# Weighing by W on three engines' paths, grouped q products and a split at column 384 in a spectral and MLP kernel

## The chip, the cores and the metric

The kernel runs on one core of one Trainium2 chip. The metric is the device time of one execution in microseconds; the time of a version is the median of several executions.

The core has a matrix engine (TensorE, PE in the profile, with its weight loads as PEld), a vector engine (VectorE, DVE), an engine for activations (ScalarE, ACT), GpSimd (POOL) and an engine that only issues transfers here (SyncE, SP). Matrix products land in PSUM, which has 8 banks of 128 partitions by 512 float32 columns. DVE and ACT copy them from there into the on-chip memory SBUF; GpSimd does not take operands from PSUM in this kernel.

## The reference

x has 2048 rows (S) and 512 columns (D), in bfloat16. Two kinds of layer, A and B, run twice in turn.

```
def _A_ref(x, w_r, w_i):
    X = rfft2(x)                     # over S and D
    X = X * (w_r + 1j * w_i)         # the weighing by W
    return irfft2(X)

def _B_ref(x, w1, w2, w3, w4):
    h = gelu(layernorm(x) @ w1)
    hs = shifted(h) @ w2             # four column groups, rows shifted by -1, +1, -2, +2
    x1 = x + hs
    return x1 + gelu(layernorm(x1) @ w3) @ w4

x = x + A(layernorm(x)); x = x + B(layernorm(x))
x = x + A(layernorm(x)); x = x + B(layernorm(x))
```

w1 and w2 are 512 by 512, w3 is 512 by 1792, w4 is 1792 by 512.

## The kernel before, in words

Row s of x is kept as partition p and index q, s = 16 p + q, so there are 16 blocks q of 128 rows. The state x stays in SBUF. The Fourier transforms are products with tables: `O` (front) transforms over p, `d` over the columns, `q` over q, then each coefficient is weighed by W (`p`), and `b`, `D`/`C` and `P` go back over q, over the columns and over p. `take` steps, one after each product, copy PSUM to SBUF: `G`/`L` after `O`, `t` after `d`, `x` after `q`, `m`/`l` after `b`, `Y` after `D`/`C`. They are `activation` copies on ACT or casts on DVE.

The spectrum is cut into 16 blocks b. Blocks 2 to 13 go through d, q and p in pairs (a unit of two), blocks 0, 1, 14 and 15 alone. A pair's d, q products, their copies (TV and X) have 1024 columns, a single's have 512. The weighing reads X and W from SBUF and writes 2048 products (1024 for a single): each value of X by the real and by the imaginary plane of W. PB holds the result. `product_slot` gives the place; the last two units reuse places of the first. A product of the q step is over 64 partitions, two at a time side by side; all other products are over 128.

After the spectral part `a` adds to x, `s` and `r` form the statistics of the rows, `n` normalises, `T` transposes by a transfer (issued by SP), `v` and `h` are w1 and its gelu, `u` is w2, `f` adds, `k`, `R`, `o`, `U` are again squares, statistics, normalising and transposing, `E` adds to x, `w`, `g`, `W` and `A` are w3, gelu, w4 and the addition to x. In layer 1 `B`, `j`, `S`, `J`, `Q` then compute the next layer's statistics and scale the table T for each q, and `O` and `G` begin the next spectral part among the w4 products. In layer 2 `y` stores the result.

Nothing is scheduled by a tool at run time or at build time: three strings, ORDER_0 (the first front), ORDER_A (layer 1) and ORDER_B (layer 2), list every step. A letter is the step, the number its index, a last letter the engine (A for ACT, V for DVE, P for GpSimd), and .n the first PSUM bank of the product. Every engine runs its own instructions in the order in which they stand in the strings, and waits for what they read. So `p4V` is the weighing of unit 4 on DVE, and everything listed behind it for DVE waits with it. `Xn` issues n products of zeros. On POOL stand also the small instructions of the row statistics (`r`, `c`, `R`, and `M`), and the issue of some table loads: `load_tables` at `f2`, and `load_rest` after ORDER_0. The first transfer of `load_rest` doubles the first quarter of W.

The last rows of w4's products are cut in two halves of 256 columns (HALVES, `columns`): in layer 1 row index 14 (W14 and W24), in layer 2 row index 10 (W10 and W20).

The weighing before (line 577) and the cut (line 740):

Of the kernel before, what the change touches and what calls it, by code (L numbers as in the profile page):

```python
# [522 lines left out]

def layer(K, last):
# [52 lines left out]
    def weigh(u, eng):  # L577
        n = len(UNITS[u])
        small = n == 1 and u not in LATE[last]
        pab[u] = t = product_slot(PB, n_pab, small, n)  # L580
        (nc.vector if eng == "V" else nc.gpsimd).tensor_tensor(t, X.pop(u)[:, 0:2 * n].unsqueeze(1).to_broadcast([P, 2, 2 * n, 256]),  # L581
                                K.W[:, :, 2 * u:2 * u + 2 * n, 1:257], op=ALU.mult)

# [156 lines left out]
    def columns(n):  # L740

        if n not in (HALVES[last], HALVES[last] + 10):
            return n, slice(0, D)
        return HALVES[last], slice(0, D // 2) if n == HALVES[last] else slice(D // 2, D)

    def w4(n):
        r, d = columns(n)
        g, i = divmod(r, 4)
        ps["W", n] = o = banks(K, 1)[:, 0, 0:d.stop - d.start]
        for t in range(14):  # L750
            nc.tensor.matmul(o, lhsT=gT[g][:, t, i * P:(i + 1) * P], rhs=K.w4[:, t, d],  # L751
                             start=(t == 0), stop=(t == 13))

    def add_x2(n):
        r, d = columns(n)
        x = K.x[:, ROWS[r], d]
        nc.vector.tensor_tensor(x, ps.pop(("W", n)), x, op=ALU.add)  # L757
# [107 lines left out]
D3.1 C3 Y0V P3.6 P2.0 a3 P0.3 a2 a0 D2.5 P1.4 Y3A C2 a1 s3 s2 D5.1 C5 P7.0 s0 P6.3 Y2V P4.4 s1 r0 Y5A a7 D6.6 a6 e0 i0
M0 C6 P5.5 D7.0 s7 C7 a4 P11.4 s6 P10.2 Y6A P12.3 n1V n0V a5 s4 s5 r1 n2V n3V T0 D4.6 C4 a10 a11 Y7A P15.5 P14.2 e1 i1
Y4A P8.1 M1 n7V n4A n6V n5V s10 c0 T1 a8 P13.4 a12 s8 P9.6 a9 s11 a15 s9 a14 v0.0 h0 r2 c2 T3 v1.6 n11V h1 n8V T2 n9V
v3.2 n10V T5 v2.0 a13 h3 u0.3 s14 h2 u3.2 c1 f3 s15 u1.5 T4 u2.4 s12 s13 f0 k0 v5.1 f1 E1V r3 c3 E3V n14A n12V n13V
n15V T6 v4.6 f2 h5 T7 u4.0 h4 u6.2 f4 E2V f6 k2 k3 E0V k1 R0 u5.1 u7.5 f7 f5 k4 E4V k6 E6V v6.2 h6 v7.5 k7 o1V h7 k5
R1 o3V E5V o2V u15.7 o5A o0V f15 k15 E7V u8.0 f8 u14.1 f14 E8V U1 u12.6 f12 k12 U0 u13.4 f13 E13V u10.0 o4V o7A U2 k14  # L870
k13 o6V f10 E10V u11.3 f11 R3 k10 U3 w0.6 k8 k11 u9.0 f9 E9V o13V k9 E12V o12V U6 w2.2 E14V g2 o14A w4.0 R2 g4 o10A g0
w3.2 E15V w5.0 g5 E11V w6.4 g6 o15V g3 w1.0 g1 w8.6 W1.3 o11V W3.2 W0.0 o9V o8V A1 B1 j1 A3 B3 W2.1 w10.2 j3 g8 A0 B0
A2 j0 B2 j2 w13.6 S0 Q1A Q0V w7.4 Q2A Q3V g10 w12.0 U7 g7 O0.4 g12 U5 G0A w9.2 g9 w11.0 U4 G0V O1.2 g13 g11 W5.5 G1A
A5 B5 w15.6 G1V I1V I0V W6.0 W7.1 A6 B6 W4.3 j5 w17.4 A7 g15 g17 w14.0 B7 j7 w18.5 A4 g18 w16.2 B4 g16 w19.4 j4 j6 S1
Q4V Q6V Q7V O3.2 Q5V g14 g19 w20.6 g20 W10.0 A10 B10 G3A G3V O2.5 j10 I3V G2A W9.4 A9 B9 j9 W11.1 A11 G2V B11 j11 W8.0
w23.2 A8 g23 w21.6 g21 w27.0 B8 j8 w22.5 S2 Q10V Q9V g27 Q8V Q11V I2V w24.2 O4.0 g22 g24 G4A w26.5 g26 w25.2 g25 G4V
I4V W12.6 A12 B12 W13.3 W15.7 j12 S12 J12 A13 B13 j13 W24.3 S13 Q12V J13 Q13V A15 B15 W14.1 j15 A24 O5.2 B24 S15 J15
A14 B14 j14 Q15V G5A S14 O6.0 J14 O15.4 G6A Q14A O14.6 L6A L15A G14A G5V I5V G15A L14A
# [5 lines left out]
b7.6 m9A m12A m5V b14.2 b6.3 V12.7 m8A V14.0 m11V m10A m14A m6A V15.1 l15A m7V D3.2 l13A D2.4 l12V l14V C3 C2 D1.6 Y2V
C1 Y3A P7.1 a7 P6.0 a6 Y1A D0.2 s7 C0 Y0A s6 P4.1 a4 s4 P5.7 a5 P2.6 P3.1 s5 a3 s3 r1 D4.2 P0.7 a2 P1.1 s2 D7.4 a0 C7
C4 a1 e1 i1 s0 D5.0 C5 Y4A s1 M1 n4V D6.6 n5V C6 r0 n6V Y6A P8.3 P9.2 e0 n7V Y5V P10.6 P12.7 i0 a9 Y7A T2 P13.0 T3 M0
n2A n0V n1V T0 P11.1 s9 P15.2 a8 s8 n3V c0 a10 s10 a11 s11 P14.4 r2 a15 v3.5 v2.1 c1 a12 h3 T1 a13 a14 v0.3 h2 c2 n10V
h0 s13 v1.6 h1 u3.5 n11V s15 n8V s14 n9V s12 f3 k3 E3V u1.4 f1 u0.0 E1V u2.3 f2 k1 T5 T4 v5.6 r3 v4.2 k2 f0 h5 u4.0 k0
n13V n12V h4 E0V n15V T6 n14V f4 k4 u7.6 f7 R0 E4V c3 u6.1 f6 o3A u5.7 f5 E5V o1A E7V k7 E2V k5 T7 E6V v6.4 h6 o0V U0
v7.0 h7 k6 R1 u14.5 f14 k14 o2A u12.0 o4A f12 u8.1 U1 f8 E8V k12 o7V u10.4 f10 o5A u15.7 f15 k10 u13.0 k15 f13 u11.1  # L890
E10V k13 R3 k8 E14V u9.5 w2.2 o6A g2 w0.6 f11 E15V E12V E13V o13A w5.1 f9 U2 w6.4 o15A g0 o12V U3 k11 k9 g5 R2 w1.6 g1
w3.0 g3 w4.2 g4 E11V U6 g6 W0.0 W2.4 o11V W3.1 W1.5 o8V o14A U7 E9V w22.2 o10A g22 o9V U4 U5 w23.6 g23 A0 y0 w24.2 g24
A3 A1 w11.0 A2 y2 y1 w7.6 g7 w12.2 w21.4 g11 y3 w27.0 g21 w26.4 w9.6 g26 w8.4 g9 g12 w25.6 g8 g25 g27 W14.2 W15.4 A15
# [33 lines left out]
```

## Time and profile before

| what | us |
|---|---|
| median of 3 runs | 347.03 (346.26 to 347.15) |
| the profiled execution | 346.95 |
| its span, first to last instruction | 345.0 |
| PE busy | 337.0 (2191 matmuls) |
| PEld busy | 188.2 |
| DVE busy | 175.8 |
| ACT busy | 197.4 |
| POOL busy | 60.8 |
| granted TensorE clock | 0.999 |

The execution's stages in the trace, with the busy time of three engines in each:

| stage | from, to | length | DVE | ACT | POOL |
|---|---|---|---|---|---|
| load of x, first front | 0 to 19.2 | 19.2 | | | |
| layer 1: d, q, weighing, b | 19.2 to 38.1 | 18.9 | 17.30 | 17.89 | 4.59 |
| layer 1: D, C, P | 38.1 to 52.6 | 14.5 | 12.63 | 12.66 | 3.74 |
| layer 1: MLP, next front | 52.6 to 179.5 | 126.9 | 63.36 | 60.95 | 22.89 |
| last front of layer 2 | 179.5 to 183.4 | 3.9 | 3.39 | 3.29 | 0.00 |
| layer 2: d, q, weighing, b | 183.4 to 202.1 | 18.7 | 17.44 | 16.87 | 0.00 |
| layer 2: D, C, P | 202.1 to 216.7 | 14.6 | 11.64 | 13.14 | 3.94 |
| layer 2: MLP | 216.7 to 341.5 | 124.8 | 35.96 | 58.56 | 18.91 |
| last addition and store | 341.5 to 345.0 | 3.5 | 0.42 | 0.00 | 0.00 |

How to read it. An engine's busy time is the time in which one of its instructions was running. The end of a matmul is modelled in the profile, and neighbours overlap, so that PE's busy time covers short gaps. A chain of waits is followed back from the last instruction to what released each step. Instructions of ACT and DVE that follow each other directly overlap a little: what one costs its engine is the distance between two starts, which is shorter than its duration. The two stages of d, q, weighing and b are called the spectral stages below.

### The profile page before, as it was taken

The numbers are of one execution on the slowest core, as the hardware profiler recorded it, in microseconds if no ns is written. First come the engines' busy times: TensorE is split into PE (matmuls) and PEld (weight loads), VectorE is DVE, ScalarE is ACT, GpSimd is POOL, SyncE is SP. The second block draws the span as 40 slices with busy tenths as digits, with TensorE's granted clock in tenths as the row PEclk, the third lists the DMA queues.
The fourth block names the chain that finished last, engine by engine and source line by source line (L and its number), as shares of the span: only waits on it lengthen the run. The fifth ranks groups of instructions, "written<-read, shape, count | busy, mean of one in ns | idle before, by whom it ended". The sixth has DMA issues, their size and how long they took to land.

```text
span 345.0 us, 5696 instructions
## 1 busy us (share of the span) xinstructions
PE 337.0 (98%) x2191; PEld 188.2 (55%) x2191; DVE 175.8 (51%) x421; ACT 197.4 (57%) x361; POOL 60.8 (18%) x157
## 2 busy tenths in 40 slices
...
DMA packets 45258, 24.59 MB, mean 71 GB/s; under 512 B 34944, under 2 KB 42240, under 8 KB 45232
## 3 DMA queue, kind: packets, MB, share of 16 engines
...
q8 instruction: 17, 0.28, 0.3%
q10 hardware_dynamic: 240, 0.10, 0.1%
...
## 4 chain that ended last, share of the span: by engine, by line
PE 80%; ACT 12%; DMA 3%; DVE 2%; issue 2%; SPq 0%; ACTq 0%; DVEq 0%
PE ps L751 28%; PE ps L731 28%; PE ps L696 8%; PE ps L680 7%; PE ps L403 3%; ACT hT L154 3%; ACT xn L290 3%; ACT X L154 3%; ACT Y L154 2%; PE ps L612 1%; ACT TV L154 1%; DMA T<-tab_T 1%; DMA x_state<-in_A_x_dram 1%; PE ps L550 1%; DMA xT<-xn 1%
## 5 line engine op out<-in xcount | busy, mean ns | idle before, releaser
L738 ACT ACTIVATE gT<-ps 128x1024 bf16<-128x1024 f32 x56 | 55.8, 1022 | 87.8 <-PE ps L731 78.1
L731 PE MATMUL ps<-xT,w 128*128 128x512 bf16 x448 | 99.0, 379 | 0.0
L751 PE MATMUL ps<-w,gT 128*128 128x512 bf16 (+1 forms) x476 | 98.6, 366 | 0.0
L757 DVE TENSOR_TENSOR x_state<-ps,x_state 128x512 bf16<-128x512 f32 (+1 forms) x34 | 22.2, 659 | 115.4 <-PE ps L751 115.4
L751 PEld LDWEIGHTS <-gT 128*128 128x128 bf16 x476 | 46.5, 98 | 50.1
L731 PEld LDWEIGHTS <-w 128*128 128x128 bf16 x448 | 43.7, 98 | 52.1 <-DMA xT<-xn 0.2
L704 DVE SCALAR_TENSOR_TENSOR xn<-xn,ln_c,ps 128x512 bf16<-128x512 bf16 x32 | 23.2, 745 | 12.6 <-PE ps L696 7.2
L680 PE MATMUL ps<-xT,w 128*128 128x512 bf16 x128 | 28.8, 379 | 0.1
L696 PE MATMUL ps<-w,hT 128*128 128x512 bf16 x128 | 28.9, 379 | 0.0
L278 DVE BATCH_NORM_STATS2 ln_st<-x_state 128x6 f32<-128x512 bf16 (+1 forms) x31 | 20.4, 668 | 4.4 <-DMA x_state<-in_A_x_dram 3.9
L290 ACT ACTIVATE junk<-xn 128x512 bf16<-128x512 bf16 x32 | 19.8, 622 | 3.2 <-DVE xn L704 3.2
L648 DVE SCALAR_TENSOR_TENSOR x_state<-ps,x_state 128x512 bf16<-128x512 f32 x32 | 20.5, 686 | 0.9 <-PE ps L640 0.8
L696 PEld LDWEIGHTS <-hT 128*128 128x128 bf16 x128 | 12.4, 98 | 15.4 <-ACT hT L687 0.8
L680 PEld LDWEIGHTS <-w 128*128 128x128 bf16 x128 | 12.3, 98 | 15.2 <-DMA xT<-xn 0.9
L290 ACT ACTIVATE xn<-x_state 128x512 bf16<-128x512 bf16 x32 | 19.9, 627 | 0.7 <-DVE x_state L648 0.4
L581 DVE TENSOR_TENSOR PB<-X,W 128x2048 bf16<-128x2048 bf16 (+1 forms) x20 | 19.4, 1009 | 0.4 <-ACT X L154 0.2
L296 POOL TENSOR_SCALAR ln_mv<-ln_s 128x4 f32<-128x4 f32 x16 | 5.1, 317 | 80.2 <-DVE x_state L648 74.1
L687 ACT ACTIVATE hT<-ps 128x512 bf16<-128x512 f32 x32 | 17.2, 601 | 1.1 <-PE ps L680 1.0
L592 PE MATMUL ps<-TR,PB 128*128 128x128 bf16 x256 | 16.5, 219 | 0.1
L640 PE MATMUL ps<-Y,Tinv 128*128 128x256 bf16 x128 | 16.1, 272 | 0.4 <-ACT Y L154 0.3
L612 PE MATMUL ps<-G,hT 128*128 128x256 bf16 x128 | 15.6, 273 | 0.3 <-ACT hT L154 0.2
L592 PEld LDWEIGHTS <-PB 128*128 128x128 bf16 x256 | 14.7, 98 | 2.1 <-issue 1.5
...
## 6 DMA issues: line engine op xcount, KB each, us to landing
w<-in_B_w_dram SPq DMA_DIRECT2D x2, 1792.0 KB, 14.5
...
```

What stands on the lines that cost most here:

```text
L154: K.nc.scalar.activation(dst, src, ACT.Copy, bias=0.0, scale=1.0)
L278: self.K.nc.vector.bn_stats(self.st[i][:, int(k)], src)
L290: K.nc.scalar.activation(out, src, ACT.Square, bias=0.0, scale=D ** -0.5, accum_out=self.s[:, i, 1:2])
L592: nc.tensor.matmul(o[:, k0 * P:(k0 + 1) * P], lhsT=pab[u][:, k, 2 * (b - u) + h, f * P:(f + 1) * P], rhs=K.TR[:, k:k + 2, 2 * b + h], star ...
L648: nc.vector.scalar_tensor_tensor(K.x[:, q, :], ps.pop(("P", q)), 1.0, K.x[:, q, :], op0=ALU.mult, op1=ALU.add, accum_out=ln[g].s[:, i, 0:1])
L680: nc.tensor.matmul(o[:, i], lhsT=K.w1[:, t, j * P:(j + 1) * P], rhs=xT[g][:, :, t, :], start=(t == 0), stop=(t == 3))
L696: nc.tensor.matmul(o, lhsT=K.hT[:, j, st:st + P], rhs=K.w2[:, j, :], start=(j == 0), stop=(j == 3))
L704: nc.vector.scalar_tensor_tensor(xn[:, q, :], xn[:, q, :], ln[q // 4].c[:, q % 4:q % 4 + 1], ps.pop(("u", n)), op0=ALU.mult, op1=ALU.add, ...
L731: nc.tensor.matmul(o[:, i], lhsT=K.w3[:, c, t * P:(t + 1) * P], rhs=xT3[g][:, :, c, :], start=(c == 0), stop=(c == 3))
L738: nc.scalar.activation(gT[g][:, 2 * j:2 * j + 2, :], ps.pop(("w", k)), ACT.Gelu_apprx_tanh, bias=0.0, scale=1.0)
L751: nc.tensor.matmul(o, lhsT=gT[g][:, t, i * P:(i + 1) * P], rhs=K.w4[:, t, d], start=(t == 0), stop=(t == 13))
L757: nc.vector.tensor_tensor(x, ps.pop(("W", n)), x, op=ALU.add)
```

## The change

The weighing gets a third form. With the letter D it reads the q product straight from PSUM on DVE, once for each block of the unit, and the copy X of that unit falls away. The letter P, which the code had, puts the weighing of X on GpSimd. The cut of the last rows moves from column 256 to 384, in both layers. Then all three orders are new.

```
@@ weigh @@
         pab[u] = t = product_slot(PB, n_pab, small, n)
+        if eng == "D":
+            o = ps.pop(("q", u))
+            for i in range(n):
+                nc.vector.tensor_tensor(t[:, :, 2 * i:2 * i + 2], o[:, :, i * 256:(i + 1) * 256].unsqueeze(1).to_broadcast([P, 2, 2, 256]),
+                                        K.W[:, :, 2 * (u + i):2 * (u + i) + 2, 1:257], op=ALU.mult)
+            return
         (nc.vector if eng == "V" else nc.gpsimd).tensor_tensor(t, X.pop(u)[:, 0:2 * n].unsqueeze(1).to_broadcast([P, 2, 2 * n, 256]),
                                 K.W[:, :, 2 * u:2 * u + 2 * n, 1:257], op=ALU.mult)
@@ columns @@
-        return HALVES[last], slice(0, D // 2) if n == HALVES[last] else slice(D // 2, D)
+        return HALVES[last], slice(0, CUT[last]) if n == HALVES[last] else slice(CUT[last], D)
@@ constants @@
 HALVES = (14, 10)
+CUT = (384, 384)
@@ ORDER_0 @@
-s1 s0 i1 i0 s3 S0 s2 s5 J0 Q1A Q0A s7 i2 i3 s4 S1 J1 O0.4 s9 f2 s6 Q2V i7 i4 i6 s10 Q3A O1.0 S2 J2 G0A Q4V s11 s8 Q5A
-i10 O2.2 i11 Q6A f3 Q7A O3.6 i8 S3 s12 J3 Q10V s13 i12 G2A Q11A i13 O5.4 s14 Q8A S4 J4 G3A Q9V s15 G5A O4.2 Q12V i14
-Q13V O6.6 L5A i15 S5 J5 Q15V O8.4 Q14V G4A G6A L6A O7.2 G7A L7A G1V G8V L8V
+s1 s0 i1 i0 S0 s2 s5 J0 Q0A Q1A s4 s7 s6 i4 f2 O0.4 i7 i6 S2 s3 J2 i2 s9 Q6V Q7V O3.0 i3 s11 S1 J1 s10 Q4A Q2A Q5A G3A
+s8 i11 i10 i8 s12 f3 O2.2 Q3P O1.6 S3 J3 Q11P s13 i12 Q10A O5.0 s15 G0A i13 Q8A Q9P S4 G2A s14 i15 J4 Q12V i14 O4.4 S5
+J5 Q15V G1A G5V Q13P O6.2 L5A O8.0 Q14V O7.6 G4A G6V G7A L7A G8V L6V L8V
@@ ORDER_A @@
-d0.6 d2.0 N0 d1.4 t0A q0.2 t1A d4.6 t2V x0A t4A p0V q1.4 q2.0 d10.2 d6.6 x1A q4.4 t10A x2V d8.0 q10.2 t6A p1V x4V
-d14.6 p2V t8A q6.4 x10A q8.0 p4V b3.7 d12.2 x6A b0.4 t14A m3V d15.7 b4.5 p6V t12A q12.2 b5.6 t15V x8A b2.7 m4A m0A m5A
-p10V q14.0 x14A b7.5 b1.6 x12A b10.4 m10A b6.0 m6A q15.1 p8V b11.3 p14V x15A b14.4 m1A p12V m7A V12.0 b9.1 m9A m2V
...
+d2.2 t2V d0.6 t0A d1.0 d4.4 N0 q0.6 t1A q2.2 d6.0 x0V p0V q1.6 t4A q4.4 x2A d10.2 t6A d8.0 p1D b1.6 p2P t10A b0.7
+q10.2 p4D m0V t8A q6.0 d14.4 m1A d12.6 x10A t14V p10V x6A d15.2 t12A p6V b2.5 b4.3 m4A q14.0 q12.6 x14A q8.3 p12D b3.0
+m2A b10.1 b11.5 x8A b7.4 t15A p14P q15.2 b5.6 b14.7 m10A b6.1 m11A b12.5 m7A m5A m3A b13.4 m6A p8V b8.6 m12A p15D b9.0
...
+a3 s3 P6.0 a2 s2 P1.1 P0.6 a1 a0 s1 P7.2 D2.4 C2 D5.6 s0 a7 s7 D7.2 C5 Y2V P5.1 r0 e0 i0 a6 Y5A a5 D4.4 s6 s5 P4.0 M0
+n3V a4 n0V n2P s4 n1P D6.6 C7 C6 Y6A P11.0 T1 C4 P10.1 Y7V P15.2 r1 e1 a11 P12.3 i1 M1 n7V T0 Y4A n6V s11 n5A T3 P13.6
...
+u6.5 f1 k1 u5.6 c2 E3V f7 E7V E2V f4 k2 R0 o2V f6 o3A v6.2 h6 v7.0 h7 f5 E1P E6V o1P k4 E0V o0V u12.4 k6 k7 k5 R1 U1
+o7A u9.5 u15.3 f9 U0 u13.1 f12 E12V u10.7 k12 E4P u14.0 u11.5 o6P U3 E5V o5A f15 u8.2 w0.3 k15 E9P g0 f8 k8 o4P f11
...
+A3 B3 g8 W2.0 R2 A2 B2 o9P o10A W1.5 W0.0 g7 A1 B1 o11A U5 o8A j1 E15V U4 w14.2 g14 w11.4 w12.2 g11 w9.4 w10.6 g9 j2
...
+W12.3 A12 B12 j12 S12 S13 J13 Q13P J12 W15.1 A15 B15 j15 S15 J15 Q15A W14.2 W24.5 Q12A Q10V O5.6 A14 A24 O6.2 G5A B14
@@ ORDER_B @@
-X5.0 d15.0 t15V d1.3 d4.4 d12.0 t4A q15.6 t1V x15A d8.2 q4.4 t12V q1.6 t8A d2.0 p15V x1V b15.2 t2V p1V d0.3 x4A q12.6
-d10.4 m15A t0A q0.0 x12A q2.2 t10A p4V b1.6 x0V p0V m1A d6.4 p12V q8.0 b4.6 x2A d14.7 t14V q10.2 t6A q6.4 b5.7 m4A
...
+X3.4 d4.1 d15.0 t15V d12.5 d1.7 t4A q4.0 t1V t12A q15.2 d0.4 d2.6 p15D x4A q1.0 d8.2 t0A q0.4 t2A t8A q2.6 p1D x0A
+q12.0 x12A d10.2 q8.4 p2D d14.0 p4P b4.1 d6.6 p12V m4V t10A x8A b3.2 b5.5 q10.3 t6A t14A q6.6 m5A b12.0 m3A b2.1 m12A
+b1.5 p8V b8.0 p0P b9.2 x6A b0.6 b15.7 m8A p10D q14.3 m1A p6V m9A p14D b11.0 m2A b10.2 m0A b6.1 b7.6 b14.3 m11A m10V
...
+m14V b13.0 V12.5 m6A V13.1 V15.4 m15A m13V V14.7 l15V m7A D3.2 l13A l12A l14A D2.0 C2 Y2A C3 Y3V D1.5 C1 P5.1 Y1A a5
+s5 P4.4 P6.0 P7.5 a4 s4 a6 s6 a7 s7 D0.6 C0 D6.0 C6 P2.2 Y0V r1 P3.3 D7.4 Y6A a2 P1.6 P0.2 e1 D4.0 s2 P12.7 a3 i1 C4
+C7 a1 a0 M1 n4V s3 D5.2 C5 s1 n5P s0 r0 T2 P13.6 Y4A n6V n7V T3 P8.1 Y7V e0 i0 M0 Y5A a8 n2A P14.4 n3V s8 P11.2 a11
...
-A5 W6.3 y5 A6 g20 W4.0 y7 y6 w16.1 g16 A4 w18.6 g18 W9.2 A9 W11.0 A11 W8.1 y11 A8 y4 y9 W20.3 y8 A20 y20 W10.7 A10 y10
+g19 A6 W7.4 A7 W5.5 y3 y7 A5 y5 y15 g14 W8.7 A8 y6 W11.4 y8 A11 W9.0 A9 y11 y9 W10.4 A10 y10 W20.1 A20 y20
```

The counts of steps by engine that the orders change:

| step | layer 1 before | layer 1 after | layer 2 before | layer 2 after |
|---|---|---|---|---|
| p, weighing | 10 DVE | 4 DVE, 4 D, 2 GpSimd | 10 DVE | 3 DVE, 5 D, 2 GpSimd |
| x, copy of the q product | 8 ACT, 2 DVE | 5 ACT, 1 DVE | 8 ACT, 2 DVE | 5 ACT |
| t | 8 ACT, 2 DVE | 8 ACT, 2 DVE | 5 ACT, 5 DVE | 8 ACT, 2 DVE |
| groups of q products in a row | 8 | 5 | 7 | 6 |
| E | 16 DVE | 10 DVE, 6 GpSimd | 16 DVE | 12 DVE, 4 GpSimd |
| o | 12 DVE, 4 ACT | 3 DVE, 7 ACT, 6 GpSimd | 6 DVE, 10 ACT | 4 DVE, 6 ACT, 6 GpSimd |
| n | 14 DVE, 2 ACT | 12 DVE, 1 ACT, 3 GpSimd | 15 DVE, 1 ACT | 10 DVE, 3 ACT, 3 GpSimd |
| Q | 13 DVE, 3 ACT | 4 DVE, 5 ACT, 7 GpSimd | | |

In ORDER_0, 4 of the 16 Q steps go to GpSimd.

More of the change, by code (lines that the diff above doesn't have):

```diff
@@ L859 @@
+J5 Q15V G1A G5V Q13P O6.2 L5A O8.0 Q14V O7.6 G4A G6V G7A L7A G8V L6V L8V
 """
 ORDER_A = """
-d0.6 d2.0 N0 d1.4 t0A q0.2 t1A d4.6 t2V x0A t4A p0V q1.4 q2.0 d10.2 d6.6 x1A q4.4 t10A x2V d8.0 q10.2 t6A p1V x4V
-d14.6 p2V t8A q6.4 x10A q8.0 p4V b3.7 d12.2 x6A b0.4 t14A m3V d15.7 b4.5 p6V t12A q12.2 b5.6 t15V x8A b2.7 m4A m0A m5A
-p10V q14.0 x14A b7.5 b1.6 x12A b10.4 m10A b6.0 m6A q15.1 p8V b11.3 p14V x15A b14.4 m1A p12V m7A V12.0 b9.1 m9A m2V
-p15V b12.7 b13.2 m12A b8.6 b15.5 m11V V15.1 m13A V13.7 m8A m14V m15V V14.2 l15V D0.4 l12V l13A l14V D1.6 C1 Y1A C0
@@ L865 @@
[L865 to L878, printed above, removed]
+d2.2 t2V d0.6 t0A d1.0 d4.4 N0 q0.6 t1A q2.2 d6.0 x0V p0V q1.6 t4A q4.4 x2A d10.2 t6A d8.0 p1D b1.6 p2P t10A b0.7
@@ new lines @@
+q10.2 p4D m0V t8A q6.0 d14.4 m1A d12.6 x10A t14V p10V x6A d15.2 t12A p6V b2.5 b4.3 m4A q14.0 q12.6 x14A q8.3 p12D b3.0
+m2A b10.1 b11.5 x8A b7.4 t15A p14P q15.2 b5.6 b14.7 m10A b6.1 m11A b12.5 m7A m5A m3A b13.4 m6A p8V b8.6 m12A p15D b9.0
+m8A b15.2 m15A V12.1 m13V V13.3 l12A m14V V15.4 V14.5 m9V l15V D3.0 l14V D1.6 l13A C1 C3 D0.2 C0 Y1A P3.4 P2.5 Y0A Y3V
+a3 s3 P6.0 a2 s2 P1.1 P0.6 a1 a0 s1 P7.2 D2.4 C2 D5.6 s0 a7 s7 D7.2 C5 Y2V P5.1 r0 e0 i0 a6 Y5A a5 D4.4 s6 s5 P4.0 M0
+n3V a4 n0V n2P s4 n1P D6.6 C7 C6 Y6A P11.0 T1 C4 P10.1 Y7V P15.2 r1 e1 a11 P12.3 i1 M1 n7V T0 Y4A n6V s11 n5A T3 P13.6
@@ new lines @@
+P9.5 n4V a10 s10 P8.4 a8 s8 v1.0 a9 s9 P14.7 a13 s13 h1 v0.4 a14 T2 c0 h0 r2 n8P v3.6 h3 v2.0 h2 n9V T4 a15 c1 n10V
+n11V u0.5 a12 u3.4 u1.0 f3 u2.1 s12 f2 s14 s15 r3 n14V T5 v5.2 n15V v4.6 c3 T7 k3 h5 u4.1 n12V h4 u7.4 n13V f0 k0 T6
+u6.5 f1 k1 u5.6 c2 E3V f7 E7V E2V f4 k2 R0 o2V f6 o3A v6.2 h6 v7.0 h7 f5 E1P E6V o1P k4 E0V o0V u12.4 k6 k7 k5 R1 U1
+o7A u9.5 u15.3 f9 U0 u13.1 f12 E12V u10.7 k12 E4P u14.0 u11.5 o6P U3 E5V o5A f15 u8.2 w0.3 k15 E9P g0 f8 k8 o4P f11
+E11V k11 w4.5 g4 w3.2 f14 k14 f10 w2.4 E10P g3 E8P w5.2 w1.6 g2 E14V g5 U2 w7.2 g1 f13 k13 R3 w6.0 k9 k10 w8.5 g6 W3.7
@@ new lines @@
+A3 B3 g8 W2.0 R2 A2 B2 o9P o10A W1.5 W0.0 g7 A1 B1 o11A U5 o8A j1 E15V U4 w14.2 g14 w11.4 w12.2 g11 w9.4 w10.6 g9 j2
+w13.4 E13P g12 g10 g13 W7.1 o13V W5.2 A0 w17.4 W4.0 j3 B0 w16.6 j0 S0 Q2V Q3V A7 A4 Q1P B7 o12P W6.3 A5 A6 B6 g16 j7
+w15.0 g15 w19.2 g19 B4 w18.0 g18 g17 w20.6 j4 j6 g20 o14A B5 W11.0 j5 S1 U6 Q6V W9.1 Q4P o15P U7 A11 B11 w21.6 Q5A
+O2.2 O1.4 Q7A G1A j11 A9 B9 W8.0 G2A G2V Q0P O0.2 G1V A8 I1V I2V B8 j8 g21 w24.6 W10.1 A10 B10 j10 G0A g24 w23.6 j9 S2
+Q11P Q9P g23 w22.0 O3.4 w26.6 g22 w27.0 G3A G3V G0V g26 Q8P I3V w25.4 g27 I0V g25 W13.2 A13 B13 j13 O4.0 G4A G4V I4V
```

21 lines of the change are left out of this document (9 added, 12 removed).

## The prediction

> **What bounds the kernel now.** I read the busy table by stage first (columns: stage in us, its length, then busy us and count of PE, PEld, DVE, ACT, POOL, then TensorE's clock, DMA share, GB/s).
>
> ```profile
> 19.20:38.10 18.90, 18.52 (x260) 14.33 (x258) 17.30 (x23) 17.89 (x30) 4.59 (x7) 1.00 0.86 285
> 38.10:52.60 14.50, 14.36 (x128) 12.50 (x129) 12.63 (x37) 12.66 (x28) 3.74 (x13) 1.00 0.80 248
> 52.60:179.50 126.90, 126.90 (x636) 59.99 (x635) 63.36 (x166) 60.95 (x107) 22.89 (x55) 1.00 0.16 30
> ...
> 183.40:202.10 18.70, 18.12 (x258) 14.37 (x258) 17.44 (x22) 16.87 (x28) 0.00 (x0) 1.00 0.01 2
> ...
> 216.70:341.50 124.80, 124.66 (x592) 57.42 (x589) 35.96 (x90) 58.56 (x101) 18.91 (x49) 1.00 0.21 46
> ```
>
> PE's busy time hides gaps, since its ends are modelled; so I use spacings. In the MLP a 512-column matmul starts every 216 ns (the chain has 56 in 12.09 us), and 128 of w1 and w2 and 448 of w3 and w4 a layer make 124.4 us: those two stages have nothing to give. What the change can shorten are the two spectral stages (d, q, b), 18.5 us (19.64 to 38.13) and 18.7 us (183.36 to 202.06). Each holds 32 + 32 + 64 + 128 matmuls of 54, 108, 54 and 54 ns: 15.7 us. The rest is seen in three places of the timeline (start, us, what, idle before):
>
> ```profile
> 22.43 0.83 PE L568 MATMUL ps<-TV,TL 64*128 64x256 bf16 x12
> 23.20 0.23 PE L544 MATMUL ps<-FL,V 128*128 128x128 bf16 x1
> 26.91 1.05 PE L568 MATMUL ps<-TV,TL 64*128 64x256 bf16 x16
> 27.89 0.62 PE L592 MATMUL ps<-TR,PB 128*128 128x128 bf16 x8
> 185.11 1.02 ACT L154 ACTIVATE TV<-ps 128x1024 bf16<-128x1024 f32 x1 [1.53 <-PE ps L550]
> 187.85 1.02 ACT L154 ACTIVATE X<-ps 128x1024 bf16<-128x1024 f32 x1
> 188.76 0.39 ACT L154 ACTIVATE hT<-ps 128x256 bf16<-128x256 f32 x1
> 189.02 0.61 ACT L154 ACTIVATE TV<-ps 128x512 bf16<-128x512 f32 x1
> ```
>
> A group of q products (L568) lasts 0.10 us plus 0.055 per matmul: 12 took 0.77, 16 took 0.98. A gap of 0.09 stands before it, so each group costs 0.2 us beyond its columns. The second point is that ACT goes from one eviction to the next without idling: the spacing is 0.91 us for 1024 columns, 0.49 for 512, 0.27 for 256. DVE takes 1.14, 0.61, 0.35, and 1.13 for a weighing of 2048, 0.61 for one of 1024. With those, the first spectral stage asks 16.8 us of ACT and 16.8 of DVE, the second 16.6 and 17.1. So evictions and PE press about equally (17.3 and 17.1 us of PE with 8 and 7 groups), and ACT in the second stage idles until 185.11.
>
> **The change, part by part.** Weighings first; per layer 10 on DVE become (layer 1 / layer 2) 4 / 3 on DVE from SBUF, 4 / 5 on DVE from PSUM (D), 2 / 2 on GpSimd (P).
>
> *D.* It removes the copy X (0.91 or 0.49 on ACT) and the weighing (1.13 or 0.61). It adds one product of 1024 read from PSUM for each unit member. No such row exists; a cast of 1024 out of PSUM is the lower end, the x2 addition from PSUM (512) the upper, doubled without its fixed part:
>
> ```profile
> L152 DVE CAST X<-ps 128x1024 bf16<-128x1024 f32 x2 | 2.4, 1224 | 0.2
> L757 DVE TENSOR_TENSOR x_state<-ps,x_state 128x512 bf16<-128x512 f32 x30 | 20.6, 691 | 112.8 <-PE ps L751 112.8
> L581 DVE TENSOR_TENSOR PB<-X,W 128x2048 bf16<-128x2048 bf16 x12 | 14.3, 1223 | 0.1
> L239 POOL COPY TL<-TL 128x512 bf16<-128x512 bf16 x1 | 1.0, 967 | 0.0
> L238 POOL TENSOR_SCALAR TL<-TL 128x512 bf16<-128x512 bf16 x1 | 1.7, 1658 | 0.1
> ```
>
> 691 less 418 (its 256 form) is 273 ns per 256, so 1.24 us for 1024, a spacing of 1.14. A D of a pair costs DVE 2.28 and saves ACT 0.91; a single costs 1.14.
>
> *P.* Pairs 2 (layer 1) and 4 (layer 2) and two singles leave DVE. No two-input GpSimd row of this size exists: the copy of 512, times four, gives at most 3.9 us, more likely 3.4 with one fixed part; the scaling, times four, 6.6. The Trainium skill (GPSIMD Engine Reference, Performance versus the Vector engine) measures 4497 ns for a two-input product of 2048 and warns against GpSimd for elementwise work. I take 4.5 for a pair and 2.25 for a single, an estimate from that page and between the rows; 3.4 and 6.6 stay for the range.
>
> *Evictions after, by the same spacings:* layer 1: ACT 16.1, DVE 15.8; layer 2: ACT 16.8, DVE 14.9. In layer 2 only DVE is relieved. q groups fall from 8 to 5 and from 7 to 6: 0.6 and 0.2 us of PE.
>
> *Layer 1, followed through the new order.* Load stage: Q0 is scaled before Q1 and S0 goes before s3, so the first product starts about 8.4 instead of 8.77; but O3 (rows 6, 7) is second and needs S2, J2, Q6 on DVE behind s4, s7, s6, i4, i7, i6, s3, i2: about 10.2, when O0 ended at 9.7. The gap eats the gain: O7 ends at 19.3 (before 19.2), and d2 waits for L8 on DVE, about 20.1 for its second matmul (before 19.97). Q3, Q11, Q9, Q13 now stand on POOL ahead of the doubling of W's first quarter, which moves from 13.42 to about 16.4; that DMA took 7.0 us, so it lands about 23.3, when p0 wants it (x0 is taken at 23.2): 0 to 0.5 us, no more than 0.1 taken. Then x2 is copied at 24.1, but POOL issues DMAs until about 25.2 (in the trace until 24.82); p2 runs to 29.7. b2 reaches PE at 28.9 and waits 0.9. After it PE has 7.8 us of columns and groups left, and the last take 0.4: D starts at 38.0, before 38.13. So **-0.1**; with p2 at 3.4 us the wait goes and ACT's own work is late next: 37.3, -0.8.
>
> *A rule against it.* The Trainium skill (SBUF — State Buffer, Who interferes with whom) says that a DVE instruction with two SBUF inputs, or in its two-port mode, and a GpSimd instruction that reads SBUF exclude each other for the whole instruction. By that p10 (DVE, ready at 28.8) would wait for p2's end, 0.9 us, and p6 behind it; p12 waits for q12 until 31.9 anyway, so about 0 to 0.3 on the stage. The one overlap in the trace speaks against a block: the scaling of TR on DVE (L811, 19.51 to 20.06) began while POOL L238 ran to 19.78, and took 547 ns for 1024 columns, where 512 columns of such an instruction (L374) take 409: no wait shows in it. But that is one pair, and ends on POOL are rough. I count no wait and keep 0.3 for the range.
>
> *Layer 2.* d4 is first, so ACT starts at 184.4 instead of 185.11. p4 (GpSimd) starts when x4 is copied, 187.4, and ends 191.9; b4 reaches PE at 191.4 and waits 0.5, which costs ACT as much before t6. From 184.5, ACT's 16.8 less the three l takes (0.8, for which D does not wait) plus that 0.5 end at 201.0, D starts at 201.3, before 202.06: **-0.8**; at 3.4 us, -1.3. The shorter fill (3 for 5) frees nothing: V's evictions end at 183.58 either way.
>
> *After the spectral stages.* n2 and n1 on POOL stand between M0 and T0, and r1 behind them. 1.0 us each (copy row) to 1.7 (scaling row): T0 leaves at +10.7 to +12.1 us after D's start, lands 3.2 later, and v1 now needs it at +14.2 (D's 7.0 us of columns, 15 of 16 P's 6.6, the 0.6 of gaps that the stage has now): 0 to 1.1, taken **+0.3**. In layer 2 n5 ends before n6, n7, for which T3 waits anyway: 0. In the MLP, E, o and Q on POOL lie under w1..w4: o1 must reach U0 before w0, 7.9 us after R0 begins (its chain 2.4, E1 and o1 2.3 by the copy row, the transpose 3.2), with 10.4 us of PE between (v6, v7 at 1.73, eight u at 0.86); U5 and U4 before w14, 7.3 us after w8 (on ACT g8, o10, g7, o11, o8, then the transpose), with 12.1 us of W3, W2, W1, W0 between. Without that cover each us is a us of PE: 0, up to +0.5.
>
> *The split at 384.* The last piece in layer 2 is 128 columns: its addition 0.28 instead of 0.42, its store 32 KB (64 KB took 1.6, 128 KB 1.9): **-0.2**, less if SP is still issuing the piece before. In layer 1 DVE now has the statistics of the 384 piece behind the last addition: 0.23 + 0.5 + 0.27 + 0.2 against 0.44 + 0.44 + 0.25: 0.
>
> **Sum:** -0.1 - 0.8 + 0.3 - 0.2 = -0.8 us. The profiled execution took 346.95 (span 345.0), 0.08 under the median 347.03; from the median: **346.2**.
>
> **Rivals.** *Everything fits* (GpSimd near 3.4 us, n near 1.0): -0.8 - 1.3 + 0 - 0.2 = -2.3, about 344.8. For it: the copy row. Against: two inputs instead of one. *GpSimd is the bound*: from 4.5 us on each further us of p2 and p4 is one of PE at b2 and b4, and n and o lengthen alike. At 5.5: +0.9, +0.2, +0.8, -0.2 = +1.7, 348.7; at 6.6 about 351. It decides above some 4.9 us. For it: the scaling row, and the rule of exclusion, which lengthens whichever starts second. Against: POOL L238 has stride 2 on both sides. *The W forms work but nothing is gained*: DVE's relief in layer 2 stays idle time because ACT is late last (16.8 us against 16.6): no change, 347.0.
>
> **Numbers.** About 0.3% (1.0 us) is what a measurement of this kernel tells from no change. The forecast has 0.38 (345.2 to 347.1; faster 0.18, same 0.20), everything fits 0.23 (faster), nothing gained 0.06 (same), GpSimd the bound 0.33 (slower 0.32, same 0.01). Faster 0.41, same 0.27, slower 0.32. The range 344.5 to 349.3 leaves out the top of the last case and the tip of the second.
>
> **What would show it.** p2 and p4 on POOL: 4.5 us, and PE waiting for them at b2 and b4. D rows at 1.23 us. ACT's first TV of layer 2 near 184.4; D's first matmul at 38.0 and, less the change so far, 201.3. Five and six groups of L568. w1's first matmul waiting for xT or not. It is wrong if GpSimd's product is far from 4.5, if DVE's weighings stretch beside it, or if a stall appears inside the MLP stages.

## The result and the profile after

| | before | after |
|---|---|---|
| median, runs side by side | 346.49 us (346.24 to 347.15, 8 runs) | 345.62 us (344.91 to 346.25, 8 runs) |
| ratio to before, 95% interval | | 0.9970 (0.9957 to 0.9983) |
| profiled execution, its span | 346.95, 345.0 | 346.01, 344.2 |

The kernel became 0.87 us faster, 0.3%. The forecast was -0.8 from the median before. The two spans differ by 0.80 us, and the rest of this section shows where these came from.

The first view is the busy table by stage of the kernel after, with the columns of the table in the prediction (stage, its length, then busy us and count for PE, PEld, DVE, ACT, POOL, then TensorE's clock, DMA share, GB/s).

```profile
19.36:37.06 17.70, 17.52 (x257) 14.80 (x258) 16.23 (x20) 16.30 (x28) 9.75 (x9) 1.00 0.75 258
37.06:51.76 14.70, 14.21 (x127) 12.00 (x125) 13.15 (x33) 12.56 (x29) 5.26 (x15) 1.00 0.93 278
51.76:179.50 127.74, 126.76 (x625) 59.60 (x635) 56.46 (x142) 63.11 (x111) 41.95 (x75) 1.00 0.17 29
...
183.60:202.00 18.40, 17.82 (x257) 14.64 (x257) 15.86 (x17) 17.06 (x27) 5.50 (x2) 1.00 0.01 2
...
216.50:341.10 124.60, 124.02 (x581) 57.03 (x590) 33.15 (x80) 56.29 (x98) 28.52 (x61) 1.00 0.21 46
```

What to see: the first spectral stage lost 0.8 us (18.49 to 17.70), the second 0.34 (18.70 to 18.36), and POOL, idle before in the second, now works 5.5 us in it. The third row is longer than before: 127.74 against 126.90.

Cut at the first d, D and w1 products of each layer, the account from before to after is:

| stretch | before | after | change | forecast |
|---|---|---|---|---|
| front, to the first d | 19.64 | 19.36 | -0.28 | } -0.1 together |
| layer 1: first d to D | 18.49 | 17.70 | -0.79 | } |
| D to w1 (after: one P product of 0.43 moved behind w1's first) | 14.48 | 14.70 | +0.22, like for like +0.65 | +0.3 |
| w1 to d of layer 2 | 130.75 | 131.88 | +1.13, like for like +0.70 | 0 |
| layer 2: first d to D | 18.70 | 18.36 | -0.34 | -0.8 |
| D to w1 | 14.59 | 14.47 | -0.12 | 0 |
| w1 to the end | 128.35 | 127.73 | -0.62 | -0.2 |

The sum is -0.80. Nearly every row differs from its forecast, and the misses cancel: that the sum is right is luck. These are also two single executions. The other profiles of the new orders below show which rows are typical of them: the first spectral stage took 17.69 or 17.70 us in five of the six others with both forms (the sixth, of e8_n1V, is told there), the second 18.36 or 18.37 in all with p0 on GpSimd. The last row is not typical: in this execution TensorE did not wait inside w1 of layer 2, and eight of the ten profiles of the new orders have such a wait, of 0.32 to 0.40 us, and take 128.0 us from w1 to the end (128.3 with the cut taken back). One of them, from the run with o14 on VectorE:

```profile
219.57 3.61 PE L686 MATMUL ps<-xT,w 128*128 128x512 bf16 x16 [0.34 <-DMA xT<-xn]
```

The groups of instructions, shapes kept apart, show what the new weighings cost (busy us and mean ns after the bar):

```profile
L584 DVE TENSOR_TENSOR PB<-ps,W 128x1024 bf16<-128x1024 f32 x13 | 15.4, 1217 | 0.7 <-PE ps L568 0.5
...
L587 DVE TENSOR_TENSOR PB<-X,W 128x2048 bf16<-128x2048 bf16 x6 | 8.2, 1381 | 0.0
L587 POOL TENSOR_TENSOR PB<-X,W 128x2048 bf16<-128x2048 bf16 x2 | 7.5, 3752 | 10.6 <-ACT X L154 10.5
...
L587 POOL TENSOR_TENSOR PB<-X,W 128x1024 bf16<-128x1024 bf16 x2 | 3.8, 1918 | 3.2 <-ACT X L154 3.2
```

D takes 1217 ns (estimate 1.24 us), GpSimd's product of 2048 3752 ns (estimate 4.5, from 3.4 to 6.6). DVE's product from SBUF, the same instruction as before, rose from 1223 to 1381 ns in the mean: that row is the first sign of what follows.

The timeline of the kernel after (start, us, what, in brackets the idle time before it and what ended it) has three new waits of TensorE above 0.3 us behind the first front:

```profile
51.76 1.89 PE L686 MATMUL ps<-xT,w 128*128 128x512 bf16 x8 [0.40 <-DMA xT<-xn]
...
147.03 1.90 PE L737 MATMUL ps<-xT,w 128*128 128x512 bf16 x8 [0.50 <-DMA xT<-xn]
...
198.38 0.39 PE L568 MATMUL ps<-TV,TL 64*128 64x256 bf16 x4 [0.53 <-DVE PB L584]
```

In turn: w1 of layer 1 waits for a transpose, w21 waits for the transpose U7, and the product q14 in layer 2 waits for DVE to read q10 out of its PSUM banks. Shorter new ones are 0.17 us at d2, 0.21 in the last front of layer 2 (for a table that ACT scales) and 0.23 at w1 of layer 2 (for an addition on DVE). The wait of q14 is a price of the form D that the prediction did not name: its product holds the banks until DVE comes to it.

### The profile page after: what moved, and what is told of

It is laid out like the page before. It is cut to its first block, busy times and chain, and to the rows that moved or that the text cites. A ratio compares the mean times of both kernels' runs of the same rounds, so it can differ in the third digit from the quotient of the medians.

```text
span 344.2 us, 5699 instructions
## 1 busy us (share of the span) xinstructions
PE 335.5 (97%) x2171; PEld 187.6 (55%) x2189; DVE 165.0 (48%) x377; ACT 195.6 (57%) x357; POOL 107.1 (31%) x200
## 4 chain that ended last, share of the span: by engine, by line
PE 87%; DMA 4%; DVE 4%; ACT 2%; issue 1%; SPq 0%; POOL 0%; ACTq 0%; DVEq 0%; POOLq 0%
PE ps L737 28%; PE ps L757 26%; PE ps L686 8%; PE ps L702 8%; PE ps L598 4%; PE ps L403 3%; PE ps L618 3%; PE ps L568 2%; DMA xT<-xn 2%; PE ps L550 2%; PE ps L646 2%; DMA x_state<-in_A_x_dram 1%; DVE x_state L654 1%; ACT xn L290 1%; ACT gT L744 1%
## 5 line engine op out<-in xcount | busy, mean ns | idle before, releaser
L757 PE MATMUL ps<-w,gT 128*128 128x512 bf16 (+2 forms) x462 | 97.8, 366 | 0.7
L763 DVE TENSOR_TENSOR x_state<-ps,x_state 128x512 bf16<-128x512 f32 (+2 forms) x34 | 22.2, 659 | 124.5 <-PE ps L757 124.5
L757 PEld LDWEIGHTS <-gT 128*128 128x128 bf16 x476 | 45.5, 98 | 51.4
L278 DVE BATCH_NORM_STATS2 ln_st<-x_state 128x6 f32<-128x512 bf16 (+2 forms) x31 | 20.2, 663 | 3.9 <-DMA x_state<-in_A_x_dram 3.6
L313 POOL TENSOR_SCALAR ln_ve<-ln_mv 128x4 f32<-128x4 f32 x11 | 2.8, 257 | 54.6 <-DVE ln_mv L306 53.9
L584 DVE TENSOR_TENSOR PB<-ps,W 128x1024 bf16<-128x1024 f32 x13 | 15.4, 1217 | 0.7 <-PE ps L568 0.5
L403 PE MATMUL ps<-Tq,x_state 128*128 128x256 bf16 (+1 forms) x160 | 14.0, 246 | 1.6 <-ACT Tq L386 1.0
## 6 DMA issues: line engine op xcount, KB each, us to landing
out_dram<-x_state SPq DMA_DIRECT2D x15, 128.0 KB, 1.9
```

What stands on the lines that cost most here:

```text
L403: K.nc.tensor.matmul(dst, lhsT=K.x[:, q, c * P:(c + 1) * P], rhs=rhs, start=(j == 0), stop=(j == 3))
```

## The experiments

Theories: the form D pays because it takes a copy off ACT, or GpSimd pays because it takes work off DVE; the lost time is a block between DVE and GpSimd in SBUF, or something else; each small wait above is a cost of the kernel, or of one execution. Times are medians, ratios are to the kernel before in the same batch; the median of the kernel before was 346.48 to 346.57 in all of them. The kernel after ran in the first of these batches alone.

### The tail alone

The kernel before, with the new cut in layer 2 and its two halves in the other order.

```
+CUT = (256, 384)
-... slice(0, D // 2) if n == HALVES[last] else slice(D // 2, D)
+... slice(0, CUT[last]) if n == HALVES[last] else slice(CUT[last], D)
-W20.3 y8 A20 y20 W10.7 A10 y10
+W10.3 y8 A10 y10 W20.7 A20 y20
```

> The kernel before, with the last rows of layer 2 alone split at 384 and the wider piece multiplied first. Theory (the tail gave half of the gain): from the last matmul to the end 3.2 us or less where the kernel before needs 3.6, of which 0.14 from the addition (0.29 for 0.42) and 0.3 to 0.4 from the smaller last store; 0.4 to 0.6 us faster than before, some 346.0. Rival (the end of the store is chance, only the addition counts): 0.1 to 0.2 us, not to be told from no change.

Measured: 346.24 us against 346.57, ratio 0.9990 (0.9981 to 0.9999). So -0.33, between the two; the interval goes from 0 to -0.7.

### The cut back in the kernel after

```
-CUT = (384, 384)
+CUT = (384, 256)
```

> The kernel after, with the last piece of layer 2 cut at column 256 again (layer 1 stays at 384). The prediction's term for this cut was 0.2 us. If that holds, the time rises to 345.8; if the whole shortening from w1 of layer 2 to the end (0.62 us between the two profiles) is the cut's, it rises to 346.2; in the run with the cut alone, on top of the kernel before, 0.33 was gained, by which it would be 345.95.

Measured: 346.04 us, ratio 0.9992 (0.9984 to 1.0000): 0.42 above the kernel after. The timeline of DVE in this kernel:

```profile
...
340.52 0.42 DVE L763 TENSOR_TENSOR x_state<-ps,x_state 128x256 bf16<-128x256 f32 x1 [1.10 <-PE ps L757]
```

and in the kernel after:

```profile
340.51 0.56 DVE L763 TENSOR_TENSOR x_state<-ps,x_state 128x384 bf16<-128x384 f32 x1 [1.48 <-PE ps L757]
341.29 0.29 DVE L763 TENSOR_TENSOR x_state<-ps,x_state 128x128 bf16<-128x128 f32 x1 [0.23 <-PE ps L757]
```

The last addition takes 0.29 instead of 0.42, and from its end to the end of the span the trace has 2.65 us instead of 2.75 (spans unrounded), with a store of 32 KB instead of 64. The other pair, the kernel before and the tail alone, has 3.05 and 2.94. So in both pairs of profiles the cut is worth 0.13 us of addition and 0.1 of store, 0.2 in all, as forecast. The medians put it at 0.33 and 0.42 us; the interval of the first holds 0.2 as well. The difference between 3.05 and 2.75, two kernels with the same cut and the same 64 KB store, belongs to the new order; no run isolates it. The cut of layer 1 was not tested alone.

### One form, the other, neither: the kernel after with its forms taken back

Three kernels with the orders of the kernel after. *D alone*: GpSimd's weighings go to DVE. *P alone*: the weighings from PSUM become a copy on ACT and a weighing on DVE again. *Neither*: both.

```
D alone:   p2P, p14P, p4P, p0P   ->  p2V, p14V, p4V, p0V
P alone:   p1D                   ->  x1A p1V       (and the seven others)
neither:   both
```

In the last two the weighings p4 and p0 of layer 2 stand a little earlier, as the three buffers of X ask.

> The changed kernel with its orders and q groups, but every weighing on VectorE from SBUF again, and an activation copy of X back in front of each that read PSUM (p4 and p0 of layer 2 stand earlier). Theory (the forms give the spectral gain): the first product of D starts in layer 1 at 38.0 or later instead of 37.06, in layer 2 at least 0.5 later than 202.00; 346.3 to 347.6. Rival (grouping and the new order give it): D at 37.1 to 37.4 in layer 1, and 345.6 to 345.9.

> The kernel after, with the four weighings of GpSimd (p2, p14 of layer 1, p4, p0 of layer 2) on VectorE at the same places of the order. VectorE gets 1.14 + 0.61 us more per layer and no weighing takes 3.7 us any more. Theory (what pays is the form that reads PSUM, because it takes a copy from ScalarE): the first spectral stage, 17.70 us from the first d product to D in the kernel after, grows by 0.3 to 1.0, the second (18.36) by -0.3 to +0.3, and the time stays within 346.0 to 347.0, not slower than the kernel before by more than 0.5. Rival (what pays is VectorE's relief by GpSimd): each stage grows by 1 us or more, and the time is 347.5 or more.

> The kernel after, with the eight weighings from PSUM put back to a copy on ScalarE and a weighing from SBUF on VectorE at the same places (in layer 2 the GpSimd weighings p4 and p0 stand a little earlier, as the buffers of X ask). ScalarE gets about 3 us more per layer, VectorE about as much less. Theory (the form that reads PSUM pays): each spectral stage grows by 2 to 3 us because ScalarE, with some 19.5 us of evictions, is late; the time is 350 to 352. Rival (GpSimd's part pays): each grows by less than 1 us, the time is 346 to 347.5.

| with the orders of the kernel after | us | ratio (95%) | first, second spectral stage |
|---|---|---|---|
| neither form | 354.07 | 1.0211 (1.0186 to 1.0235) | 21.66, 22.49 |
| P alone | 357.58 | 1.0323 (1.0299 to 1.0348) | 27.08, 21.88 |
| D alone | 347.83 | 1.0038 (1.0023 to 1.0053) | 19.10, 19.13 |
| both (the kernel after) | 345.62 | 0.9970 (0.9957 to 0.9983) | 17.70, 18.36 |

Neither theory as stated holds. D alone is worth 6.2 us to these orders, which were written for it: without the forms they are 7.5 us slower than the kernel before, and no run puts D into the old orders. GpSimd without D *costs* 3.5 us, and with D it brings 2.2, so the two forms depend on each other. They do so in layer 1 only: there GpSimd's part costs the stage 5.42 us without D and brings 1.40 with it. In layer 2 it brings 0.61 without D and 0.77 with it. The reason is in the timeline of P alone, layer 1:

```profile
24.98 3.86 POOL L587 TENSOR_TENSOR PB<-X,W 128x2048 bf16<-128x2048 bf16 x1
...
25.04 4.36 DVE L587 TENSOR_TENSOR PB<-X,W 128x1024 bf16<-128x1024 bf16 x1 [1.62 <-ACT X L154]
...
29.46 1.89 PE L598 MATMUL ps<-TR,PB 128*128 128x128 bf16 x16 [4.07 <-DVE PB L587]
31.28 1.89 PE L568 MATMUL ps<-TV,TL 64*128 64x256 bf16 x16
```

DVE's product of 1024 takes 0.69 us elsewhere in that kernel. Here it began 0.06 us after GpSimd's product, lasted 4.36 us, and ended 0.56 us after GpSimd was done: nearly all of its work was still to do then. TensorE waited 4.07 us for it. In the kernel after, the same stretch has D's on DVE:

```profile
23.74 3.49 DVE L584 TENSOR_TENSOR PB<-ps,W 128x1024 bf16<-128x1024 f32 x3
...
24.05 3.88 POOL L587 TENSOR_TENSOR PB<-X,W 128x2048 bf16<-128x2048 bf16 x1
```

Three in 3.49 us, 1.16 apiece, all but the first 0.31 us beside GpSimd's product: not stretched (the prediction's spacing is 1.14). So the form that reads PSUM is what lets GpSimd work beside DVE at this place; an order that keeps p1 clear of p2 without D was not tried. This is the rule that the prediction weighed and set aside (the Trainium skill, SBUF — State Buffer, Who interferes with whom): two SBUF inputs on DVE and a GpSimd instruction that reads SBUF exclude each other, and the page says as well that a DVE instruction with at most one SBUF input, outside the two-port modes, does not contend. The runs agree with both halves. A second loss followed in P alone, seen in its table by stretch:

```profile
...
29.46:34.90 5.44, 5.44 (x44) 4.13 (x45) 2.71 (x4) 2.54 (x3) 0.00 (x0) 0.50 0.57 164
...
```

The granted clock (third number from the end) is 0.50 for 5.4 us after TensorE's 4 us of standing still: the 16 q products took 1.89 us where the kernel after has 1.05. These four executions scatter (356.98 to 358.76), and the profiled one is the longest, so the 27.08 us of its first stage may be at the upper end.

D alone shows what DVE must do in GpSimd's place, in the same order:

```profile
27.97 0.22 PE L544 MATMUL ps<-FL,V 128*128 128x128 bf16 x1 [0.88 <-DVE PB L584]
...
193.79 0.62 PE L598 MATMUL ps<-TR,PB 128*128 128x128 bf16 x8 [1.41 <-DVE PB L587]
```

The first is again a product that waits for banks which a late D still reads; the second is b4, waiting for p4 behind two D's on DVE. The two stages grew by 1.40 and 0.77.

### The block in layer 2

In the kernel after, GpSimd's p0 (second of the POOL row) lies beside DVE's p12, which reads X and W from SBUF:

```profile
187.74 5.50 POOL L587 TENSOR_TENSOR PB<-X,W 128x2048 bf16<-128x2048 bf16 x2 [10.54 <-ACT X L154]
...
189.85 2.36 DVE L584 TENSOR_TENSOR PB<-ps,W 128x1024 bf16<-128x1024 f32 x2 [0.33 <-PE ps L568]
192.13 2.20 DVE L587 TENSOR_TENSOR PB<-X,W 128x2048 bf16<-128x2048 bf16 x1
```

p12 takes 2.20 us instead of 1.22; the two D's before it, beside p4, are at their usual pace. The experiment puts p0 on DVE:

```
-b1.5 p8V b8.0 p0P
+b1.5 p8V b8.0 p0V
```

> The changed kernel, in layer 2 p0 on VectorE instead of GpSimd. Theory (exclusion: p12, which reads SBUF twice, lasted 2.20 us because GpSimd's p0 ran until 193.24): p12 takes 1.2 us, the PSUM-read p10 ends 0.3 to 0.5 earlier although VectorE has p0's 0.6 more, PE's wait of 0.53 for its banks falls to 0.1 or 0.2, D starts 0.3 to 0.5 earlier than 202.00; about 345.2. Rival (p12 was long for its data or a place in PB): p12 stays at 2.2, D starts 0.5 to 0.6 later, 346.2.

Measured: 345.48 us, ratio 0.9963 (0.9952 to 0.9973). In its timeline:

```profile
187.03 3.63 POOL L587 TENSOR_TENSOR PB<-X,W 128x2048 bf16<-128x2048 bf16 x1 [10.54 <-ACT X L154]
...
191.42 1.22 DVE L587 TENSOR_TENSOR PB<-X,W 128x2048 bf16<-128x2048 bf16 x1
...
197.31 0.39 PE L568 MATMUL ps<-TV,TL 64*128 64x256 bf16 x4 [0.26 <-DVE PB L584]
```

p12 is back at 1.22, the wait of q14 halves, and the stage falls from 18.36 to 17.99. So p0 on GpSimd, which spares DVE a product of about 0.7 us, costs the stage 0.37 us: it took 18.36 or 18.37 in the four profiles with p0 on GpSimd and both forms, and 17.99 in all three with p0 on DVE. The whole kernel's median moved by only 0.14, which the intervals do not tell from the kernel after.

### The waits for transposes

Layer 1 with n0 ahead of n3, and separately o14 on VectorE:

```
-n3V a4 n0V n2P s4 n1P                  -g20 o14A B5
+n0V n3V a4 n2P s4 n1P                  +g20 o14V B5
```

> The changed kernel, in layer 1 n0 on VectorE before n3 and a4 instead of behind them. Theory (w1 of layer 1 waits for the transpose T0, and T0 for n0): T0 is issued 0.5 to 0.8 us earlier, w1 no longer waits 0.40 for it and starts at 51.3 instead of 51.76; 0.3 to 0.4 us faster than the changed kernel, some 345.2. Rival (as predicted, n1 and n2 on GpSimd hold T0): w1 at 51.7 to 51.8, no change, 345.6.

Measured: 346.28 us, ratio 0.9984 (0.9974 to 0.9993). That is 0.66 above the kernel after, though the two intervals touch. From D to w1 the profile has 15.17 us instead of 14.70: a P product waited 0.32 for an addition on DVE, the transpose T1 left at 47.38 instead of 46.97, and w1 waited 0.55 instead of 0.40. The theory fell: w1 starts on T1, T1 waits for n3, and putting n0 in front only delays that. n3 itself takes 0.83 us on DVE beside GpSimd's n1, and 0.41 without it. The first line is from e7_best, the second from e8_n1V (both below):

```profile
46.02 0.83 DVE L374 TENSOR_SCALAR xn<-x_state,ln_mv,ln_r 128x512 bf16<-128x512 bf16 x1
...
46.54 0.41 DVE L374 TENSOR_SCALAR xn<-x_state,ln_mv,ln_r 128x512 bf16<-128x512 bf16 x1
```

> The kernel after, with one normalisation of layer 1, o14, on VectorE instead of ScalarE, where it stood behind three gelus and let the transpose U7 leave at 142.4. Theory (o14 on ScalarE makes w21 wait for U7): the 0.50 us wait of TensorE at w21 is gone and the time is 0.3 to 0.5 below the kernel after, 345.1 to 345.3. Rival (that wait belongs to the one profiled execution, where the transpose landed late, and most executions have none): the time stays within 0.15 of the kernel after, 345.5 to 345.8, whatever the profile shows at w21.

Measured: 345.37 us, ratio 0.9965 (0.9952 to 0.9978), 0.25 below the kernel after: between the two, and the intervals do not tell it from no change. In the kernel after U7 leaves late, right after o14 on ACT:

```profile
142.42 1.23 SPq L674 DMA_TRANSPOSE xT<-xn  x1
```

and with o14 on DVE at

```profile
140.27 1.23 SPq L674 DMA_TRANSPOSE xT<-xn  x1
```

with no wait at w21 any more. But the profile of the run with p0 on DVE, which left o14 on ACT, has no wait at w21 either: it stands on the edge, and only some executions pay. Of the seven profiles with o14 on ACT in the new orders three have the wait (0.50, 0.33 and 0.36), of the three with o14 on DVE none.

### Both together, and n1 on VectorE

```
e7_best:  p0P -> p0V,  o14A -> o14V
e8_n1V:   and  n3V a4 n0V n2P s4 n1P  ->  n3V a4 n0V n1V n2P s4
```

> The kernel after with two changes together: p0 of layer 2 on VectorE instead of GpSimd, and o14 of layer 1 on VectorE instead of ScalarE. Alone they gave 345.48 and 345.37 against 345.62 of the kernel after. Theory (each takes one wait of TensorE away, 0.4 at the second spectral stage and up to 0.5 at w21): 345.0 to 345.3, ratio to the kernel before 0.995 to 0.9965, and no wait at w21. Rival (the two single results are scatter around the kernel after): 345.5 to 345.7.

> The run e7_best and, in layer 1, n1 on VectorE in place of GpSimd, with n2 alone on GpSimd beside nothing of VectorE's that reads only SBUF. Theory (n3 on VectorE is held by GpSimd's n1, 0.83 instead of 0.41 us, and the transpose T1 behind it): n3 takes about 0.41, T1 leaves 0.4 us earlier, the wait of w1 for the transposes goes, and the time is 0.1 to 0.4 below e7_best. Rival (the chain a0..a7 of additions on VectorE, one of which is now 0.4 us later, takes the place of the transposes): P waits for x_state, and the time is that of e7_best within 0.1 or above it.

Measured: 344.96 us, ratio 0.9961 (0.9949 to 0.9973), and 344.72 us, ratio 0.9956 (0.9944 to 0.9967). Both are better than the kernel before, by 1.5 and 1.8 us. They are 0.7 and 0.9 us below the kernel after in the medians, with intervals that overlap its own, so that is likely and not shown; between themselves the intervals do not decide. In the second, n3 took 0.41 us, and T1 left 9.50 us after D's start instead of 9.93 in e7_best: that step is shown. The gain at w1 is not: in the profiled execution (346.19 us, one of three of the twelve above 346) T1 itself took 2.28 us instead of 1.27, and w1 waited 1.00. That execution also differs earlier:

```profile
24.04 0.62 POOL L185 DMA_DIRECT2D W<-W  x1 [2.18 <-DMA W<-in_A_w_i_dram]
...
25.45 3.87 POOL L587 TENSOR_TENSOR PB<-X,W 128x2048 bf16<-128x2048 bf16 x1
...
28.78 2.77 DVE L587 TENSOR_TENSOR PB<-X,W 128x2048 bf16<-128x2048 bf16 x2
```

p2 starts at 25.45, as the prediction had it (25.2), because POOL waits 2.18 us for W to land before it may issue a transfer that stands ahead of p2; in the kernel after it waited 0.72 and p2 began at 24.05. The last line is p10 and p6 on DVE, 2.77 us instead of 2.36: p10 began while p2 still ran, to 29.32. TensorE waited 0.48 us for banks that a late D still read and 0.25 for p2, and the stage took 18.54 us, no less than in the kernel before. With the 15.22 from D to w1 (14.55 in e7_best) that is about the 1.5 us by which this execution is longer than the usual ones. That W landed late fits all of the first part (DVE, too, waited 0.25 and 0.56 us for W), but no run isolates it. Why T1 took longer stays open, and so does whether the two other slow executions are of this kind.

## Why the prediction was right in sum and wrong in its terms

The total came out within 0.1 us by luck: layer 1 up to D and the end of layer 2 gained more than forecast, the way to w1, the MLP and the second spectral stage less. The mechanisms of D and of the split hold. What fails is the step that set the block between DVE and GpSimd aside.

**Layer 1 up to D (-0.1; measured -1.07).** D began at 37.06, not 38.0. Two sizes were off: GpSimd's product takes 3.88 us, not 4.5, and p2 began at 24.05, not 25.2, so b2 never waited. This is the case that the prediction wrote beside its sum ("with p2 at 3.4 us ... 37.3, -0.8") and the front's gain of 0.28, which it thought eaten. Of the two sizes the start matters more: from 24.05 even a product of 4.5 us would have ended before b2 came (28.8). The orders alone do not settle it, since POOL waits for W there: in the execution of e8_n1V p2 began at 25.45, b2 did wait, and the stage gained nothing. The front's start scatters by 0.7 us between the executions of all these runs (18.91 to 19.64), so that gain is not shown. The copy row of POOL, the lower end (3.9 us), was closer than the 4497 ns of the Trainium skill (GPSIMD Engine Reference, Performance versus the Vector engine), which are for an fp32 addition and not for a product in bfloat16. But that is luck in part: the 967 ns of that copy were themselves stretched, as shown below, and four times its usual 747 is 3.0.

**D to w1 (+0.3; like for like +0.65).** Right in kind, wrong in cause. The prediction's path ran over n1 and n2 on GpSimd to T0. GpSimd's n takes 784 ns, under the low end assumed, and was done by 46.76. It was DVE's n3, blocked beside it, that let T1 leave at 46.97; 0.40 us of waiting is in the profile.

**The MLP stage (0, at most +0.5; like for like +0.70).** The covers worked out for o1, U5 and U4 on GpSimd held: none of these made TensorE wait. The one that failed was not looked at: o14 on ACT behind three gelus, ahead of U7 and w21. It cost 0.50 in the profiled execution, and nothing in four of the seven with o14 on ACT. In the profiles of the new orders without that wait the stretch is, like for like, at most 0.3 us longer than before: there the forecast holds. No run takes E, o, n and Q back from GpSimd as a whole.

**Layer 2 (-0.8; measured -0.34).** ACT's earlier start came as said (1.75 us after the first d before, 1.08 after), and b4 did not wait, which by the prediction's own sum would make -1.3. The step that failed is "I count no wait": the prediction looked for the block beside p2 in layer 1 only, and beside p2 and p4 of the kernel after DVE runs D's, which are not held; in layer 2 p0 and p12 met. That cost the stage 0.37. The other loss, q14 behind p10D's banks, has 0.26 us left with p0 moved. The last 0.3 us of the miss is not accounted for.

**The witness against the block.** The prediction saw no wait in the scaling of TR on DVE, 547 ns beside POOL's L238 and L239, because 512 columns of another such instruction take 409. The new orders bring the comparison that was missing. There POOL does not compute beside the scaling of TR, and the scaling not beside POOL's copy L239:

```profile
19.45 0.75 POOL L239 COPY TL<-TL 128x512 bf16<-128x512 bf16 x1
...
21.71 0.47 DVE L817 TENSOR_SCALAR TR<-TR 128x1024 bf16<-128x1024 bf16 x1
```

Over all ten profiles of the new orders the scaling takes 0.42 to 0.50 us and the copy 0.75; in the two profiles with the old order, where they overlap, 0.55 and 0.97. So both were stretched, and the pair spoke for the block, not against it.

**The tail (-0.2; 0.2 in two pairs of profiles, 0.33 and 0.42 in their medians).** Mechanism right, and the size as well by the profiles. The -0.62 from w1 to the end is more than the cut: 0.3 us of it is the end of the store under the new order, and most executions of the new orders give 0.3 back at w1.

**The rivals.** "GpSimd is the bound" needed over 4.9 us and fell with 3.75. "Everything fits" was right about layer 1 and about the size of n (0.784 us), and wrong about layer 2. "Nothing is gained" fell with the ratio, whose interval ends at 0.9983, and with both spectral stages, which became shorter; for layer 2 alone (-0.34) it was not far off.

The form D was costed correctly (1.24 against 1.217 us) but undervalued. Without GpSimd's part it brings these orders 6.2 us, as a saving of engine time; with it 12.0 (357.58 to 345.62), because it also keeps DVE off the block.
